# A fused attention and gating kernel on one core: a new order of its units, and a last output tile in two halves

## The chip, the core and the metric

The kernel runs on one core of a Trainium2 chip. A core has five engines that run side by side: TensorE (PE, matrix products, with PEld for the loading of its weights), VectorE (DVE), ScalarE (ACT), GpSimd (POOL) and SyncE (SP). Each takes its instructions in the order in which the program has them and waits at semaphores for the others. The metric is the device time of one execution in microseconds (us), lower is better: the median of three runs.

## The reference

Sinkhorn attention over blocks, and behind it a gated MLP whose gate mixes the tokens. There are 4 batches, 8 heads, 768 tokens in 8 blocks of 96, and a head size of 64; d_model is 512, d_ff 1024.

```python
P = sort_net                                   # (4, 8, 8, 8)
for _ in range(5):                             # Sinkhorn steps
    P = exp(P - max(P, -1)); P = P / sum(P, -1); P = P / sum(P, -2)
k_sorted = einsum('bhij,bhjcd->bhicd', P, k_blocks)     # the same for v
scores = q_blocks @ k_sorted.T / sqrt(64)      # inside each block of 96
attn = softmax(scores) @ v_sorted              # -> x, (4, 768, 512)

h = relu(x @ w_in); u, v = h[..., :512], h[..., 512:]
v_n = (v - mean(v)) / sqrt(var(v) + 1e-6)
v_s = einsum('ts,bsd->btd', w_spatial, v_n) + b_spatial
out = (u * v_s) @ w_out                        # (4, 768, 512) float32
```

## The kernel before

The whole kernel is one program of units, small functions that each issue one piece of work: for most of them the matmuls into one or two PSUM banks and the copy that empties them. A string, `ORDER`, lists the units with their arguments, and `run` calls them one by one. The schedule is manual: each engine gets its instructions in the order of the string, and only semaphores hold it up. So the string sets, for every engine, what stands behind what.

The arguments of a unit are, in this order, the PSUM bank (0 to 3 stand for the bank pairs 0-1, 2-3, 4-5 and 6-7; 10 to 17 stand for the single banks 0 to 7), for units with a choice the engine that copies (A is ACT, D is DVE, P is POOL), and then the batch, the head pair and so on. The units that matter here:

- `DM:bank:n:w` issues n matmuls of w columns on a zero tile, whose results nobody reads. They stand at the start, where PE has nothing else to do.
- `SK:n` is one Sinkhorn step (ACT's exponential, then DVE); the last one also turns P into `p_t`. `MC` makes `spread` on ACT, `MA` and `MB` make the mask on DVE. `PR` multiplies `spread` and `p_t` into PSUM; `P0` (batch 0, DVE) and `PD` (the others, POOL) multiply that by the mask into `pd`, a matrix per head that mixes the blocks.
- `L:q`, `L:k`, `L:v`, `L:wv` and so on load inputs, on POOL's queue, in order. `LH` and `QC` bring half of q of batch 0 over ACT's queue.
- `KT`, `VT` mix k and v with `pd` and turn them; `QT`, `QQ` turn q; `VB` turns the mixed v of batch 0 back into `vb`. For later batches `VM` mixes v into `vm`, and `VC` moves it into `vb` by small DMAs.
- `SC` makes scores and their exponential (ACT), `AT` the weighted sum of v and its division by the row sums (DVE, lines 505 and 506). `XT` turns the result for the MLP, on PE; `XD` does that by a DMA.
- `VP`, `UP` are the two halves of `x @ w_in`, with a ReLU; `ST`, `LN`, `LA` normalise v (DVE, ACT, DVE). `WT`, `WW` turn w_spatial (one or two chunks). `SP` mixes the tokens, DVE adds the bias into `z`, `GT` multiplies by u. `OP`, `OE`, `OS` make, copy and store an output tile.
- `CK` and `CF` check that no Sinkhorn sum left the range in which the quick form holds, and `LF` loads that flag on every engine. After `IF` stands the rest of the quick path; the other branch computes everything in a general form and is not run here.
- In the last batch `SH`, `GH` do `SP`, `GT` in narrower pieces, and `OH:bank:b:n:c0:c1`, `OI`, `OJ` make, copy and store the columns c0 to c1 of one output tile of 128 tokens. `OJ` ends in S or A for SP's or ACT's DMA queue.

The front of the program, up to the first `VP`, handles the Sinkhorn steps and the attention of batch 0; from there on, units of neighbouring batches are interleaved, so that matmuls of the MLP of one batch stand between the attention units of the next.

## Time and profile before

| | |
|---|---|
| three runs | 153.0, 153.16, 153.27 us; median 153.16 |
| the profiled execution | 154.13 us, of which 152.3 us from the first to the last instruction (the span) |
| PE busy | 143.7 us (94% of the span) |
| DVE, ACT, POOL busy | 114.7 (75%), 85.0 (56%), 42.3 us (28%) |
| chain that ended last | PE 83%, DVE 10%, DMA 2% |
| HBM traffic | 24.78 MB read, 6.29 MB written |

Rows of the timeline have the start in us, the duration in us, the engine, the line of the kernel, the operation, what it writes and from what, the shapes, the count, and in brackets how long the engine was idle before it and what ended that. Rows of the chain have start, duration and what ran. Rows of the waits have who waited for whom, the total in us, how many times, and the longest. Rows of the groups have a count, then busy us and the mean ns of one, then the idle time before them.

### The profile page before, as it was taken

The page shows a single profiled execution, that of the slowest core. Times are in us where ns is not written, and L with a number is a line of the kernel's source. Part 1 is how long each engine was busy: PE and PEld are TensorE (multiplying, and loading weights), DVE is VectorE, ACT ScalarE, POOL GpSimd, SP SyncE. Part 2 cuts the span into 40 slices and gives each one's busy share as a digit, 9 for nine tenths or more (in the row PEclk, how much of TensorE's full clock was granted, in tenths as well). Part 3 has the DMA queues.
Part 4 walks back from the last instruction along what each step waited for, and adds up shares of the span by engine and source line. Part 5 has one row for each costly group of instructions (what it writes and reads, how often), then busy time and mean ns, then how long its engine had stood idle before and what let it go on. Part 6 is the DMA issues. An engine that isn't in the chain of part 4 may idle for free.

```text
span 152.3 us, 4112 instructions
## 1 busy us (share of the span) xinstructions
PE 143.7 (94%) x1687; PEld 95.9 (63%) x1687; DVE 114.7 (75%) x264; ACT 85.0 (56%) x122; POOL 42.3 (28%) x46
## 2 busy tenths in 40 slices
PE   6786999989999999999999999999999999999991
PEld 2175867764687565965786674657875546764760
DVE  1789889966978773969992785988936989886742
ACT  4274999875889806788879055776240141340040
POOL 7400997092000004625000039200000620003630
PEclk9999999999999999999999999999999999999999
DMA  3999999999999990799993989300075024019356
GB/s 102 255 204 204 185 190 205 208 214 237 240 257 205 204 185 8 118 127 197 202 163 75 230 218 285 69 0 4 0 223 126 0 108 167 0 50 403 115 189 229
DMA packets 30695, 24.38 MB, mean 160 GB/s; under 512 B 10384, under 2 KB 27792, under 8 KB 30672
## 3 DMA queue, kind: packets, MB, share of 16 engines
q0 software_dynamic: 14432, 12.19, 50.6%
q1 hardware_dynamic: 14864, 9.92, 24.5%
q10 hardware_dynamic: 1376, 1.97, 3.8%
q8 instruction: 14, 0.23, 0.6%
q14 instruction: 9, 0.07, 0.2%
HBM read 24.78 MB, written 6.29 MB: 204 GB/s over the span
## 4 chain that ended last, share of the span: by engine, by line
PE 83%; DVE 10%; DMA 2%; issue 1%; ACT 1%; DVEq 0%
PE ps L619 15%; PE ps L564 14%; PE ps L607 14%; PE ps L645 10%; PE ps L675 5%; PE ps L498 5%; PE ps L452 4%; PE ps L393 4%; PE ps L695 3%; PE ps L420 3%; PE ps L528 2%; PE ps L324 2%; DVE x_sb L506 2%; DMA p_all<-in_sort_net_dram 2%; PE ps L411 1%
## 5 line engine op out<-in xcount | busy, mean ns | idle before, releaser
L636 POOL TENSOR_TENSOR gt<-z,u_sb 128x768 bf16<-128x768 f32 x9 | 14.6, 1637 | 70.1 <-DVE z L625 27.9
L457 ACT ACTIVATE ex_all<-ps 96x768 bf16<-96x768 f32 x32 | 23.9, 805 | 5.0 <-PE ps L452 4.6
L619 PE MATMUL ps<-wspT,v_sb 128*128 128x384 bf16 x144 | 24.9, 326 | 0.0
L564 PE MATMUL ps<-w_in_sb,xT 128*128 128x512 bf16 x96 | 23.4, 380 | 0.0
L607 PE MATMUL ps<-xT,w_in_sb 128*128 128x384 bf16 x128 | 23.1, 326 | 0.0
L506 DVE TENSOR_TENSOR x_sb<-ps,rec_all 96x512 bf16<-96x512 f32 x32 | 22.0, 686 | 1.1
L625 DVE TENSOR_TENSOR z<-ps,b_bc 128x768 f32<-128x768 f32 x12 | 11.4, 953 | 13.1 <-PE ps L619 13.1
L619 PEld LDWEIGHTS <-v_sb 128*128 128x128 bf16 x144 | 13.7, 98 | 8.7
L127 ACT ACTIVATE v_sb<-ps 128x512 bf16<-128x512 f32 (+1 forms) x15 | 9.9, 657 | 15.9 <-DVE bad L722 8.7
L581 DVE BATCH_NORM_STATS2 stats<-v_sb 128x6 f32<-128x512 bf16 x24 | 16.2, 674 | 1.7 <-ACT v_sb L127 1.5
L607 PEld LDWEIGHTS <-w_in_sb 128*128 128x128 bf16 x128 | 12.1, 98 | 7.9
L645 PE MATMUL ps<-w_out_sb,gt 128*128 128x256 bf16 x144 | 16.9, 273 | 0.0
L121 ACT COPY o_sb<-ps 128x1024 f32<-128x1024 f32 (+1 forms) x10 | 8.8, 882 | 12.9 <-DVE z L681 9.0
L127 ACT ACTIVATE u_sb<-ps 128x768 bf16<-128x768 f32 x12 | 9.7, 809 | 10.3 <-PE ps L607 10.3
L645 PEld LDWEIGHTS <-gt 128*128 128x128 bf16 x144 | 13.9, 98 | 2.1
L564 PEld LDWEIGHTS <-xT 128*128 128x128 bf16 x96 | 8.4, 98 | 8.5
L498 PEld LDWEIGHTS <-ex_all 96*128 96x128 bf16 x256 | 10.7, 97 | 3.6 <-issue 0.6
L498 PE MATMUL ps<-vb,ex_all 96*128 96x65 bf16 x256 | 11.8, 193 | 0.2 <-DVE x_sb L506 0.2
L291 POOL TENSOR_TENSOR pd<-mask,prep_sb 128x512 bf16<-128x512 bf16 x6 | 6.6, 1103 | 14.4 <-ACT prep_sb L121 9.6
L688 POOL TENSOR_TENSOR gt<-z,u_sb 128x512 bf16<-128x512 f32 (+1 forms) x5 | 5.2, 1046 | 18.4 <-DVE z L681 18.4
L121 ACT CAST vm<-ps 128x768 bf16<-128x768 f32 x9 | 7.1, 807 | 4.8 <-PE ps L420 4.7
L235 PE MATMUL ps<-warm 128*128 128x256 bf16 (+1 forms) x34 | 8.1, 400 | 1.3 <-DVE warm L209 1.3
(100 smaller groups left out, 208.6 us busy)
## 6 DMA issues: line engine op xcount, KB each, us to landing
out_dram<-o_sb SPq DMA_DIRECT2D x8, 512.0 KB, 3.4
v_in<-in_v_dram POOLq DMA_DIRECT2D x4, 768.0 KB, 13.3
k_in<-in_k_dram POOLq DMA_DIRECT2D x4, 768.0 KB, 11.1
vb<-vm SPq DMA_DIRECT2D x24, 99.0 KB, 4.4
q_in<-in_q_dram POOLq DMA_DIRECT2D x3, 768.0 KB, 25.3
ws_in<-in_moe_w_spatial_dram POOLq DMA_DIRECT2D x2, 576.0 KB, 17.8
w_in_sb<-in_moe_w_in_dram POOLq DMA_DIRECT2D x2, 512.0 KB, 12.4
q<-in_q_dram ACTq DMA_DIRECT2D x1, 768.0 KB, 4.6
```

Of the source, the lines that this page charges most:

```text
L121: nc.scalar.copy(out=out, in_=in_)
L127: nc.scalar.activation(out=out, in_=in_, func=AF.Relu)
L457: nc.scalar.activation(out=e_tile(b, hp, ih).rearrange("p h (x g) -> p h x g", g=G), in_=t[0:BLK, :, 0:HW].rearrange("p h (g x) -> p h x g ...
L498: nc.tensor.matmul(t[:, hh, ii * VW:ii * VW + D + 1], lhsT=e[:, c:c + 128], rhs=vb[b % 2][:, ih * NI + ii, 2 * hp + hh, 0:D + 1], start=Tr ...
L506: nc.vector.tensor_mul(out=x_sb[:, hp].rearrange("p i (h d) -> p h i d", h=2), in0=tv[:, :, :, 0:D], in1=_raw_ap(rec, 0, [rec.ap[0], [NI, ...
L564: nc.tensor.matmul(t[:, x, :], lhsT=st["xT", b][:, n // 3, kc, (n % 3) * 128:(n % 3 + 1) * 128], rhs=w_in_sb[:, kc, DH:DFF], start=(kc == ...
L581: nc.vector.bn_stats(out=stats, in_=st["v_sb", b, n])
L607: nc.tensor.matmul(t[:, x, 0:HW], lhsT=w_in_sb[:, kc, mc * 128:(mc + 1) * 128], rhs=st["xT", b][:, ih, kc, :], start=(kc == 0), stop=(kc = ...
L619: nc.tensor.matmul(t[:, x, 0:HW], lhsT=st["v_sb", b, n][:, mc * 128:(mc + 1) * 128], rhs=wspT[:, 3 * x:3 * x + 3, n, :], start=(n == 0), s ...
L625: nc.vector.tensor_add(out=z.rearrange("p (x c) -> p x c", x=2), in0=t[:, :, 0:HW], in1=b_bc.rearrange("p (x c) -> p x c", x=2),)
L636: eng.tensor_mul(out=gt, in0=st["z", b, mc], in1=u)
L645: nc.tensor.matmul(t[:, x, c:c + w], lhsT=st["gt", b, mc][:, (n0 + x) * 128:(n0 + x + 1) * 128], rhs=w_out_sb[:, mc, c:c + w], start=(mc = ...
```

## The change

All units stand in a new order, with other PSUM banks and, for many, another engine for the copy. Counted over the string: 16 of 16 `UP` are copied by ACT (12 before), 10 of 22 `VP` units by DVE (7 before), 5 of 6 `WT` by DVE, where before there were two `WT` and two `WW`, all on ACT; one `KT` and one `VM` go from DVE to ACT, one `VB` from ACT to DVE (all four are there now). The first `DM` units have 13 matmuls of 256 columns and 4 of 512, in place of 12 of 512; those between q's turning and `PR` have 8 of 512 and 9 of 256, in place of 18 of 256 (and 4 behind `PR`, now none). On POOL's queue k of batch 1 is loaded ahead of v of batch 1, and both, with q of batch 1, ahead of the first two `PD`. Four of the `VC` DMAs of the last batch and two more output stores go over ACT's queue.

The last output tile's columns 0 to 256 are made, copied and stored as 0 to 128 and 128 to 256, the first copied by ACT and stored over ACT's queue, the second by DVE and SP. The function for `VP` gets an argument `parts`, and a unit `VH` that uses it is added, but no unit of the order calls it.

The new string, cut to its front and its end, and the rest of the diff:

```diff
-S0 CO DM:10:5:512 IV:0 LH:A:0 TB SK:0 DM:10:3:512 L:q:0:4:8 BH ID SK:1 SK:2 IV:2 QC:A:0 DM:10:4:512 QC:A:1 SK:3 MA
-L:v:0:0:8 MC SK:4 QQ:0:A:0:0 DM:12:10:256 DM:12:8:256 L:k:0:0:8 QT:12:D:0:3 PR:13 L:v:1:0:8 MB DM:10:4:256 P0:0:2
...
-OJ:3:5:256:512:S OJ:3:4:0:256:A
+S0 CO DM:10:6:256 L:q:0:4:8 L:v:0:0:8 LH:A:0 TB SK:0 BH ID SK:1 SK:2 DM:10:7:256 DM:10:2:512 QC:A:0 QC:A:1 SK:3
+DM:10:2:512 SK:4 QQ:0:A:0:0 MC IV:0 MA QT:12:A:0:3 DM:13:8:512 MB DM:13:9:256 PR:10 P0:0:2 P0:2:4 P0:4:6 P0:6:8
...
+OH:10:3:4:128:256:0:4 OI:D:3:4:128:256 OJ:3:5:256:512:S OJ:3:4:0:128:A OJ:3:4:128:256:S
...
-    def u_VP(ps, eng, b, *tiles):
+    def u_VP(ps, eng, b, *tiles, parts=1):
...
-            for kc in range(KC):
-                nc.tensor.matmul(
-                    t[:, x, :],
...
+            for c in range(0, DH, DH // parts):
+                for kc in range(KC):
+                    nc.tensor.matmul(
+                        t[:, x, c:c + DH // parts],
...
+    def u_VH(ps, eng, b, *tiles):
+        u_VP(ps, eng, b, *tiles, parts=2)
```

## The prediction

> **What bounds the kernel now.** I read the windows view first, cut where the work changes character, then the waits of VectorE (DVE) in the first cut, then the timeline and the chain at the places that the new order touches.

> The windows view, with busy us and (in brackets) instructions of each engine, then clock, DMA share and GB/s:

> ```profile
> core 0: us, PE busy (x) PEld busy (x) DVE busy (x) ACT busy (x) POOL busy (x), PEclk, DMA share, GB/s
> 12.98:33.11 20.13, 18.39 (x431) 14.91 (x430) 18.24 (x35) 17.04 (x24) 13.21 (x15) 1.00 1.27 199
> 33.11:148.94 115.83, 115.81 (x1185) 75.96 (x1181) 88.11 (x189) 62.09 (x89) 24.50 (x20) 1.00 0.69 149
> 148.94:152.25 3.31, 0.00 (x0) 0.00 (x0) 0.43 (x2) 0.00 (x0) 0.00 (x0) 1.00 0.59 212
> ```

> The kernel has three parts. From 33.11 to 148.94 us TensorE (PE) is busy 115.81 of 115.83 us: no order of the same matmuls can shorten that stretch, and a bad one can only open holes. Before it lies a front of 33.11 us, in which PE is held up by others; behind it 3.31 us in which the last copies and stores land. A gain must come from the front or the end.

> In the front the Sinkhorn steps run first, to 12.4; they are the same in both kernels. In the cut behind them three columns lie close together: of 20.13 us DVE is busy 18.24, ScalarE (ACT) 17.04, PE 18.39. A busy PE there holds many short matmuls that overlap, so I take DVE, which cannot overlap much, as the engine that paces it. Its last copies before the steady stretch are at the very end of the cut:

> ```profile
> 32.23 0.33 PE L528 MATMUL ps<-ident,x_sb 96*128 96x96 bf16 x4 [0.45 <-issue]
> 32.60 0.56 DVE L123 COPY xT<-ps 128x768 bf16<-128x768 bf16 x1 [0.43 <-PE ps L528]
> 33.11 3.19 PE L564 MATMUL ps<-w_in_sb,xT 128*128 128x512 bf16 x14
> ```

> So DVE ends the front at 33.16, PE begins its long run at 33.11, and DVE was idle 20.13 - 18.24 = 1.89 us on the way. The waits of DVE in this cut, and the instructions that stood behind them:

> ```profile
> DVE vb L123 <- PE ps L411: 0.5, 2, 0.3
> DVE xT L123 <- PE ps L528: 0.4, 1, 0.4
> DVE rec_all L505 <- PE ps L452: 0.4, 1, 0.4
> DVE vt_all L123 <- PE ps L393: 0.3, 1, 0.3
> 15.60 0.69 DVE L123 COPY vb<-ps 96x1024 bf16<-96x1024 bf16 x1 [0.29 <-PE ps L411]
> 17.43 1.81 DVE L123 CAST kt_all<-ps 128x768 bf16<-128x768 f32 x2
> 19.43 1.28 DVE L123 COPY vb<-ps 96x1024 bf16<-96x1024 bf16 x2 [0.19 <-PE ps L411]
> 21.66 0.35 PE L452 MATMUL ps<-qT,kt_all 64*128 64x96 bf16 x8 [0.21 <-DVE x_sb L506]
> 22.01 0.20 DVE L505 RECIPROCAL rec_all<-ps 96x8 f32<-96x8 f32 x1 [0.40 <-PE ps L452]
> 46.95 1.02 DVE L123 COPY xT<-ps 128x768 bf16<-128x768 bf16 x2
> ```

> **Term 1, the front.** First what the order shows on DVE in the first half of the front, before (pd is the block-diagonal mix matrix, vt_all and kt_all the mixed v and k, vb the turned v, rec_all and x_sb the normalised output of one attention unit AT):

> ```order
> L279 TENSOR_TENSOR pd<-mask_89,ps 128x256 x4
> L123 CAST vt_all<-ps 128x768
> L123 COPY vb_97<-ps 96x8x2x64
> L123 CAST vt_all<-ps 128x768
> L123 CAST kt_all<-ps 128x768 x2
> L123 COPY vb_97<-ps 96x8x2x64 x2
> L505 RECIPROCAL rec_all<-ps 96x8
> ```

> Before, one vb copy stands between the vt_all casts and two behind the kt_all casts. The same place on DVE after:

> ```order
> L280 TENSOR_TENSOR pd<-mask_89,ps 128x256 x4
> L124 CAST vt_all<-ps 128x768
> L124 COPY vb_97<-ps 96x8x2x64 x2
> L124 CAST vt_all<-ps 128x768
> L124 CAST kt_all<-ps 128x768 x2
> L124 COPY vb_97<-ps 96x8x2x64
> L506 RECIPROCAL rec_all<-ps 96x8
> ```

> Now two stand between the vt_all casts, and one is left before the first AT; the fourth vb copy (ACT did it) comes later on DVE. In the second half DVE loses one kt_all cast to ACT and gains one xT copy. Its work changes by -1.81/2 + 1.28/2 + 1.02/2 = -0.91 + 0.64 + 0.51 = +0.2 us. The mask's reduction and cast, and the q copy that leaves DVE, lie ahead of 12.98.

> Then the idle time. Only 0.40 + 0.27 (the vt_all row, 0.3) + 0.19 + 0.43 + 0.29 of it has a named cause. The 0.40 was a ring: the scores' matmuls at 21.66 waited for banks that the AT before held, and the next AT stood behind them in PE's queue. In the new order the first three ATs go to banks 6-7, 4-5 and 0-1, and two of them wait in PSUM while DVE works on the first: I strike 0.40. The vt_all wait is covered by the second vb copy: 0.27 off. The vb wait of 0.19 goes too, for its matmuls no longer come right behind two casts with nothing between. The 0.29 stays, since the first vb still hangs on ACT's cast of the first vt. The 0.43 comes from a hole of 0.45 us in PE's own stream ("issue") that no unit explains; I strike half, 0.2. Left are 1.89 - 0.40 - 0.27 - 0.19 - 0.2 = 0.83 us, and DVE would end the front at 12.98 + 18.24 + 0.2 + 0.83 = 32.25 in place of 33.16: 0.9 earlier. Ends of the range: nothing gained (the waits come back elsewhere and the 0.2 is added: +0.2), or no idle time at all: 31.4, 1.7 earlier.

> One thing cuts this short. The heads' v of the second batch goes through vm and eight small DMAs into vb, and the first AT of that batch needs four of them (the second row is the fourth DMA alone, issued at 31.75):

> ```profile
> 29.52 5.41 SPq L433 DMA_DIRECT2D vb<-vm  x8
> vb<-vm SPq DMA_DIRECT2D x1, 99.0 KB, 7.9
> 42.29 0.48 PE ps L498 x16
> 97.08 0.86 PE ps L564 x4
> 97.95 1.30 PE ps L607 x8
> ```

> The fourth landed at 31.75 + 7.9 = 39.65, and the AT ran at 42.3, so nobody waited. In the new order that AT stands behind six VP tiles (0.86 each), two SC and one UP (1.30), some 7.0 us after the run starts: at 32.25 + 7.0 = 39.3. The last vm copy also comes some tenths earlier, with the front. I let this eat 0.3: the front is worth **-0.6 us**.

> **Term 2, the steady stretch.** Counted by unit from the two orders, the matmuls are the same in number and shape, but for the last tile. There 4 of 256 columns become 8 of 128. A row for 128-column matmuls with their own 128-column weights each (the transposes of the spatial weights) gives their pace, 0.67/12 = 0.056, so 0.45 in place of 4 x 0.109 (16 of 256 columns in 1.75): +0.01.

> ```profile
> 41.62 0.67 PE ps L541 x12
> 74.23 1.75 PE ps L645 x16
> ```

> Everything else here is hidden while PE has its next operands. More copies go to ACT (all 16 of u; busy 62.09 of 115.83) and to DVE (88.11): both have room. Four vb DMAs of the last batch are now issued by ACT (about 0.68 each, 5.41/8), at a place where ACT has only casts behind them; three output stores join them. The front's loads keep their bytes. The order of POOL's queue shows v0 ahead of k0 in both kernels; what changes is k1 ahead of v1, and that k1, v1 and q1 are no longer queued behind the two pd products that wait for ACT. The transfers run at 199 GB/s through the front, so the stream of loads has no gap to close and I cost that at nothing; cover gone, it would be a few tenths at the first use of v1. Sum of term 2: **0**, to +1 where a margin fails (rivals).

> **Term 3, the end.** The chain's last pieces, the stores' issues and their landing, and the copies' sizes:

> ```profile
> 149.01 0.42 DVE o_sb L123
> 148.16 1.65 ACTq L707 DMA_DIRECT2D out_dram<-o_sb  x3
> DMA to landing us min/median/max: 1.8/2.2/2.7
> L123 DVE COPY o_sb<-ps x5: 424/425/693, 146.4 to 149.0; 128x256 f32<-128x256 f32 x4, 128x512 f32<-128x512 f32 x1
> ```

> Now: the copy of 256 columns ends at 149.43, ACT issues its store at 149.47 (the third of the row, 0.34 long), it lands 1.8 later. The order of ACT's last rows before:

> ```order
> L121 COPY o_sb<-ps 128x512 x2
> L707 DMA out_dram<-o_sb 128x512
> L121 COPY o_sb<-ps 128x512
> L707 DMA out_dram<-o_sb 128x256 x3
> L803 UNCONDITIONAL_BRANCH
> ```

> The last three stores stood together, with no copy between them. After, the same rows of ACT from the third copy on:

> ```order
> L122 COPY o_sb<-ps 128x512
> L712 DMA out_dram<-o_sb 128x256 x2
> L122 COPY o_sb<-ps 128x128
> L712 DMA out_dram<-o_sb 128x128
> L808 UNCONDITIONAL_BRANCH
> ```

> ACT now copies the first half itself behind its second store; DVE copies the other half, and SP stores it. DVE's 693 for 512 and 425 for 256 columns put 128 at about 0.29 (an estimate on their line): 149.01 + 0.29 = 149.30, SP's issue at 149.34 in place of 149.47. ACT's half comes out at the same moment. **-0.1 us**, from -0.2 to +0.4 (landing in 2.2, the median, with five stores in flight, not 1.8).

> **The sum.** -0.6 + 0 - 0.1 = -0.7. The profiled execution took 154.13 with a span of 152.3; it would be 153.4, span 151.6. It lies 0.97 above the median of the three runs (153.16); against that the forecast is **152.5 us**. About 0.2% (0.3 us) is what a measurement of this kernel can tell from no change.

> **Rivals.** *A, slower: the warm-up matmuls come too late or too few.* The rows:

> ```profile
> PEclk9999999999999999999999999999999999999999
> 1.28 5.30 PE L235 MATMUL ps<-warm 128*128 128x512 bf16 x12 [1.28 <-DVE warm L209]
> 7.85 0.53 PE L324 MATMUL ps<-ident,q_in 128*64 128x128 bf16 x12 [1.27 <-ACT q_in L121]
> 9.04 2.14 PE L235 MATMUL ps<-warm 128*128 128x256 bf16 x18
> 12.40 0.35 PE L265 MATMUL ps<-p_t,spread 32*128 32x32 bf16 x8 [0.76 <-DVE p_t L260]
> ```

> The first twelve took 5.30/12 = 0.44 per 512 columns, the later ones 2 x 2.14/18 = 0.24: PE's pace doubled between 6.6 and 9.0, though the granted clock (first row, by slices of 3.8 us) reads full from the start. The new order has 5376 columns ahead of q's transposes, not 6144, so they end at 1.28 + 5.30 x 0.875 = 5.9, and PE then idles 1.9 us to 7.85, not 1.27. Behind the transposes it puts 6400 columns ahead of the matmuls (L265) that P waits for, not 4608: at the fast pace 2.97 us, ending near 12.4, just when p_t is ready; at the slow pace 5.52 us and slower transposes, ending near 16. If PE is still slow then, the whole front moves by up to 3.5 us, and by about 1.2 if the pace doubles halfway; I take +1.7 on the forecast, 154.2. It decides as soon as the dummies end after 12.5. For it: the margin is nil. Against: 4.6 us of work is still a long stretch. [...] Chance **0.14**.

> What spread, the other operand of these matmuls, waits for, and the first product behind them:

> ```profile
> 8.75 0.60 ACT L226 COPY spread<-ident 32x512 bf16<-32x512 bf16 x1
> 10.51 1.41 ACT L121 COPY qT<-ps 128x1536 bf16<-128x1536 bf16 x1
> 12.98 1.41 DVE L279 TENSOR_TENSOR pd<-mask,ps 128x256 bf16<-128x256 bf16 x4
> ```

> A smaller delay of the same matmuls is sure: ACT now makes spread (L226, 0.60) behind the copy of qT (1.41), not ahead of the last exponential; 10.51 + 1.41 + 0.60 = 12.5, against the 12.40 at which p_t released PE. P's first product (L279) started at 12.98 before, behind the mask's cast, so at most 0.1 of it shows.

> *B, no change: the front's gain is handed back.* DVE keeps its 1.89 us of idle time in other places, or the first AT of the second batch waits for vb until 39.65 and longer: 153.1. [...] Chance **0.20**.

> The rows for rival C, z's sums, the first and the last of the check's instructions, and its matmul:

> ```profile
> L625 DVE TENSOR_TENSOR z<-ps,b_bc 128x768 f32<-128x768 f32 x12 | 11.4, 953 | 13.1 <-PE ps L619 13.1
> 119.17 0.41 DVE L721 TENSOR_REDUCE ends<-rec_all 96x1 f32<-96x256 f32 x1
> 120.85 0.14 DVE L722 TENSOR_SCALAR bad<-ends 32x1 bf16<-32x1 f32 x1
> 124.85 0.10 PE ps L735
> ```

> *C, slower by holes in the steady stretch.* The check of the sums (CK, short DVE instructions from 119.17 to 120.99) and its matmul (CF) stood 3.8 us apart. Now DVE adds z of the last SP (0.96), runs CK (1.8), and PE passes OP (1.75) and UP (1.30) meanwhile: 3.05 against some 3.0 with the latency. DVE behind by half a us there stops PE for as long, as would the six normalising products ahead of the next-to-last batch's SP, where I count 0.3 of room. Two such holes of 0.5 and a front that gains nothing: 154.1, and slower by any sum over 1.0. Chance **0.12**.

> **How the numbers follow.** The forecast, 152.5, has 0.54; its own range is 151.9 (the front at 1.2) to 153.0. Low end of all: 151.9; the high end takes in rivals C and the middle of A: 154.2. Faster: 0.54 x 0.95 + 0.20 x 0.25 = 0.56. Slower: A 0.14, most of C 0.11, a quarter of B 0.05 = 0.30. The same: 0.14.

> **What would show it.** Right: PE's long run (first L569) begins near 32.4, DVE's idle time from the first pd product to there is near 0.9, PE has no hole behind it, and the last store is issued 0.1 earlier after the last matmul. Wrong: dummies that take 0.44 per 512 columns behind the transposes (A); a wait of PE on vb, or a start at 33 (B); waits of PE on DVE near CF or before an SP (C).

## The result, and the profile after

The first comparison gave the changed kernel 154.72 us (median of four runs, 154.44 to 155.07) against 153.13 for the kernel before: 1.0105 times as long, with a 95% interval of 1.0082 to 1.0128. The forecast was 152.5, the upper end of its range 154.2. More executions on another chip, below, put the change nearer to nothing (1.0029, 0.9996 to 1.0062). Why the two differ is half of the story: with the new order, PE has half clock for 3.4 us at the head of some executions (3 of 4 in the first comparison, 4 of 11 in the second) and not of the others. Two executions far above the rest (156.0 us of the changed kernel, 156.3 us of the one without a branch) are left out of all counts and medians here and below.

The profiled execution of before was late at its head: its first exponential, which waits for the Sinkhorn input, began 0.72 us later than in another execution (at 3.31, not 2.59), and all behind it followed. So that other one (same kernel, span 151.2) is compared here.

**The head.** The timeline of the changed kernel, warm-up, q's transposes, warm-up, and the spread matmuls on which P hangs:

```profile
1.28 4.41 PE L236 MATMUL ps<-warm 128*128 128x256 bf16 x17 [1.28 <-DVE warm L210]
7.17 0.53 PE L325 MATMUL ps<-ident,q_in 128*64 128x128 bf16 x12 [1.48 <-ACT q_in L122]
9.09 4.16 PE L236 MATMUL ps<-warm 128*128 128x512 bf16 x16 [0.33 <-issue]
13.18 0.36 PE L266 MATMUL ps<-p_t,spread 32*128 32x32 bf16 x8
```

The same places of the kernel before:

```profile
1.28 4.51 PE L235 MATMUL ps<-warm 128*128 128x512 bf16 x12 [1.28 <-DVE warm L209]
7.14 0.53 PE L324 MATMUL ps<-ident,q_in 128*64 128x128 bf16 x12 [1.35 <-ACT q_in L121]
8.33 2.14 PE L235 MATMUL ps<-warm 128*128 128x256 bf16 x18
11.68 0.35 PE L265 MATMUL ps<-p_t,spread 32*128 32x32 bf16 x8 [0.76 <-DVE p_t L260]
```

The spread matmuls come at 13.18, not 11.68, and nothing but the warm-up ahead of them on PE holds them up (p_t was ready at 11.66, spread at 11.76). By windows (PE busy first; the granted clock is the third figure from the end), the changed kernel:

```profile
8.00:10.00 2.00, 1.67 (x27) 1.07 (x29) 1.31 (x7) 0.50 (x3) 0.00 (x0) 0.68 1.31 204
10.00:12.00 2.00, 2.00 (x6) 0.68 (x5) 1.76 (x9) 2.00 (x3) 0.00 (x0) 0.50 1.31 203
12.00:14.00 2.00, 1.54 (x18) 1.17 (x17) 0.49 (x3) 0.45 (x1) 0.00 (x0) 0.97 1.31 204
```

A mean of 0.68, 0.50 and 0.97 is half clock for 1.28 + 2.00 + 0.12 = 3.4 us, from 8.7 to 12.1. The 16 warm-up matmuls took 4.16 us; in a kernel below, at full clock, the same 16 take 2.66.

**The rest, by parts.** From the spread matmuls to the long run of matmuls (first VP), to the first OH, to the end of the last matmul, to the end; the changed kernel, then the kernel before:

```profile
13.18:33.11 19.93, 18.43 (x437) 15.24 (x436) 18.18 (x36) 15.98 (x23) 11.35 (x13) 1.00 1.28 206
33.11:143.24 110.13, 109.71 (x1146) 72.83 (x1150) 82.91 (x183) 60.24 (x86) 25.03 (x19) 1.00 0.73 147
143.24:148.97 5.73, 5.53 (x38) 3.17 (x35) 3.11 (x8) 1.76 (x3) 1.41 (x2) 1.00 0.30 112
148.97:153.27 4.30, 0.01 (x1) 0.00 (x0) 0.31 (x2) 0.27 (x1) 0.00 (x0) 0.86 0.64 226
```

```profile
11.68:32.03 20.35, 18.96 (x441) 15.44 (x440) 18.73 (x37) 17.04 (x24) 12.85 (x15) 1.00 1.28 201
32.03:142.49 110.46, 109.93 (x1146) 72.94 (x1151) 84.90 (x182) 60.34 (x86) 23.44 (x18) 1.00 0.72 149
142.49:147.85 5.36, 5.36 (x34) 3.03 (x31) 3.22 (x8) 1.75 (x3) 1.40 (x2) 1.00 0.45 170
147.85:151.17 3.32, 0.00 (x0) 0.00 (x0) 0.45 (x2) 0.00 (x0) 0.00 (x0) 1.00 0.60 213
```

Head +1.50, front -0.42, steady stretch -0.33, last tiles +0.37, end +0.98: +2.1 us. The front did become shorter, and the head and the end took 2.85 us for the 0.75 that it and the steady stretch gave.

**The end.** The chain of waits of the changed kernel at that place:

```profile
144.36 0.09 DVE gt L693
144.46 2.56 issue
...
147.19 0.70 DVE o_sb L124
147.89 0.04 issue
147.93 0.61 PE ps L700 x4
```

"issue" is DVE with nothing to execute, and it comes right behind its branch (`IF`): its next instruction follows the branch by 2.64 us, before by 1.84. So DVE copies the third output tile at 147.19, 3.95 us after the first OH; before it was 2.84 after, and PE ended the wait:

```profile
145.33 0.69 DVE L123 COPY o_sb<-ps 128x512 f32<-128x512 f32 x1 [1.42 <-PE ps L695]
```

PE needs that bank again: from one matmul's start to the next 0.48 us pass there in place of 0.11, a hole of 0.37 us (the windows view has 0.20 idle, since the ends of matmuls are modelled). And the stores come late and all at once. The DMA engines (last figure GB/s) are idle, then full to the end:

```profile
147.50:148.00 0.50, 0.30 (x4) 0.12 (x2) 0.50 (x2) 0.00 (x0) 0.00 (x0) 1.00 0.06 16
148.00:148.50 0.50, 0.50 (x7) 0.45 (x7) 0.50 (x2) 0.00 (x0) 0.00 (x0) 1.00 0.00 0
150.50:151.00 0.50, 0.00 (x0) 0.00 (x0) 0.00 (x0) 0.00 (x0) 0.00 (x0) 1.00 1.11 387
```

Last, the program's final waits on SP (start of the first and of the last), changed kernel, then before:

```profile
L837 SPq EVENT_SEMAPHORE  x8: 27/28/28, 151.9 to 152.3; - x8
```

```profile
L832 SPq EVENT_SEMAPHORE  x5: 28/28/28, 149.3 to 150.2; - x5
```

In the semaphore records there is one wait for each of the eight semaphores that the stores share, always in the same order, 0.06 us apart. Eight stores leave the last one at the end of that order. The ninth takes the first place: when it lands at 151.87, seven waits still follow, to 152.31. The last of all landings, the eighth store's, is at 152.05, so 0.24 us are lost to the order. Before, the last wait came 0.02 behind the last landing.

### The profile page after: what moved, and what is told of

It is laid out like the page before. It is cut to its first block, busy times and chain, and to the rows that moved or that the text cites. A ratio compares the mean times of both kernels' runs of the same rounds, so it can differ in the third digit from the quotient of the medians.

```text
span 153.3 us, 4096 instructions
## 1 busy us (share of the span) xinstructions
PE 143.5 (94%) x1682; PEld 96.6 (63%) x1691; DVE 112.0 (73%) x265; ACT 84.8 (55%) x123; POOL 44.2 (29%) x47
## 4 chain that ended last, share of the span: by engine, by line
PE 80%; DVE 8%; issue 4%; ACT 3%; POOL 2%; ACTq 0%; DVEq 0%
PE ps L624 15%; PE ps L566 14%; PE ps L612 14%; PE ps L650 10%; PE ps L499 5%; PE ps L453 4%; PE ps L394 3%; PE ps L236 3%; PE ps L421 3%; PE ps L680 3%; PE ps L325 2%; PE ps L529 2%; POOL gt L693 2%; PE ps L535 1%; PE ps L412 1%
## 5 line engine op out<-in xcount | busy, mean ns | idle before, releaser
L641 POOL TENSOR_TENSOR gt<-z,u_sb 128x768 bf16<-128x768 f32 x10 | 16.4, 1644 | 69.7 <-DVE z L630 64.8
L566 PE MATMUL ps<-w_in_sb,xT 128*128 128x512 bf16 x88 | 22.7, 380 | 0.4
L128 ACT ACTIVATE u_sb<-ps 128x768 bf16<-128x768 f32 x16 | 12.8, 809 | 12.2 <-PE ps L740 8.7
L122 ACT COPY o_sb<-ps 128x1024 f32<-128x1024 f32 (+2 forms) x12 | 10.0, 842 | 12.3 <-PE ps L700 9.3
L650 PEld LDWEIGHTS <-gt 128*128 128x128 bf16 x144 | 13.9, 98 | 2.4
L122 ACT CAST vm<-ps 128x768 bf16<-128x768 f32 x10 | 7.7, 806 | 10.0 <-PE ps L421 10.0
L122 ACT CAST kt_all<-ps 128x768 bf16<-128x768 f32 x11 | 8.4, 801 | 4.9 <-PE ps L394 4.9
L128 ACT ACTIVATE v_sb<-ps 128x512 bf16<-128x512 f32 (+1 forms) x12 | 7.9, 670 | 5.3 <-PE ps L566 5.1
L292 POOL TENSOR_TENSOR pd<-mask,prep_sb 128x512 bf16<-128x512 bf16 x6 | 6.5, 1096 | 13.2 <-ACT prep_sb L122 9.1
L236 PE MATMUL ps<-warm 128*128 128x256 bf16 (+1 forms) x33 | 8.6, 440 | 1.6 <-DVE warm L210 1.3
## 6 DMA issues: line engine op xcount, KB each, us to landing
k_in<-in_k_dram POOLq DMA_DIRECT2D x4, 768.0 KB, 13.1
w_in_sb<-in_moe_w_in_dram POOLq DMA_DIRECT2D x2, 512.0 KB, 12.4
```

The costliest lines, as they stand in the source:

```text
L122: nc.scalar.copy(out=out, in_=in_)
L128: nc.scalar.activation(out=out, in_=in_, func=AF.Relu)
L236: nc.tensor.matmul(t[:, 0, 0:int(w)], lhsT=warm[:, 0:128], rhs=warm[:, 0:int(w)], start=True, stop=True)
L566: nc.tensor.matmul(t[:, x, c:c + DH // parts], lhsT=st["xT", b][:, n // 3, kc, (n % 3) * 128:(n % 3 + 1) * 128], rhs=w_in_sb[:, kc, DH + c ...
L641: eng.tensor_mul(out=gt, in0=st["z", b, mc], in1=u)
L650: nc.tensor.matmul(t[:, x, c:c + w], lhsT=st["gt", b, mc][:, (n0 + x) * 128:(n0 + x + 1) * 128], rhs=w_out_sb[:, mc, c:c + w], start=(mc = ...
```

## The experiments

Theory: three separate causes, half-clock windows (head), a late copy behind DVE's branch (end), a ninth store (end). The rival to each stands in the expectations. Diffs are against the changed kernel, except where said.

### How much of it is chance: both kernels again

> The kernel before, unchanged, run again for its profile, the spans of several executions and their granted clock. Its timed runs lie at 153.0 to 153.27 us, but its profiled execution took 154.13 (span 152.3). Theory 1: that one execution was a slow one by about 1 us at its start or its end; other executions should show spans near 151.3 and the same steady stretch, and the microsecond should be found in the head (the long run of matmuls starting before 33.1) or behind the last matmul (under 3.31 us). Rival: the profiled execution is like the others and a profiled run costs 1 us by itself; then every span of it is near 152.3.

Measured: spans of 151.2 to 151.7 in twelve executions; the profiled one was the fastest. The first theory holds: the missing 1.08 us lie ahead of the long run (from 32.03, not 33.11), 0.72 of them in the head (spread matmuls at 11.68, not 12.40).

> The changed kernel, unchanged, in more executions. Theory of the clock: the windows in which the clock is granted begin at a point of their own in every execution; where a window of 3.41 us covers the idle time of PE between 5.7 and 7.2 us, the next one is granted half, the granted clock of the run is 0.982 to 0.987 and its time is 1.1 to 1.3 us longer. So the times fall into two groups about 1.2 us apart, by the granted clock, and the better group lies near 154.0 to 154.4 (0.8 to 1.1 us above the kernel before, all of it at the end). Rival: the granted clock and the time have nothing to do with each other, and the times form one group around 154.7.

Measured: 1.0029 (0.9996 to 1.0062). By granted clock the executions split as said, but the better group lies lower than expected, at 153.59 and not at 154.0 to 154.4, and one of it (154.45) stands between the groups. Here and below, "half" counts those with a granted clock of 0.989 or less:

| kernel | executions | half | median half | median others |
|---|---|---|---|---|
| before (five chips, 129 in all; medians of the chip of the next row) | 129 | 11 | 154.61 | 153.32 |
| changed, again | 11 | 4 | 154.90 | 153.59 |
| changed, first comparison | 4 | 3 | 154.79 | 154.44 |
| before, 1.5 fewer warm-up matmuls | 12 | 6 | 154.13 | 153.37 |
| all kernels here with the changed kernel's own warm-up | 80 | 38 | | |
| all kernels here with four more warm-up matmuls | 30 | 0 | | |

So the first comparison met three half executions in four, and an execution of that kind costs some 1.3 us more. The others of the second are only about 0.3 us above the kernel before; the single other one of the first, 154.44, is not explained.

### The warm-up

```diff
-DM:10:2:512 SK:4 QQ:0:A:0:0 MC
+DM:10:6:512 SK:4 QQ:0:A:0:0 MC
```

> The changed kernel with four more warm-up matmuls of 512 columns ahead of q's transposes (the last group is 6 instead of 2). Theory (rival A of the prediction): after the change PE idles from 5.7 to 7.2 us, the clock is granted at half from 8.7 to 12.1 us, the warm-up behind the transposes therefore ends at 13.18 instead of under 12.4, and the spread matmuls start 0.78 us late. With PE busy to about 6.7 the clock should stay full: granted clock of the run near 1.0, spread matmuls at 12.4 to 12.5, the long run of matmuls from 32.4 instead of 33.1, time 0.6 to 0.8 us under the changed kernel. Rival: the half clock comes from something else than the idle time, and it stays; then the time is the same or up to 0.2 us longer.

Measured: 1.0068 (1.0055 to 1.0080), no half execution in six, spread matmuls at 11.81 and the long run from 31.69, earlier than expected (12.4 was where P was ready in the late execution of before):

```profile
8.92 2.66 PE L236 MATMUL ps<-warm 128*128 128x512 bf16 x16 [0.16 <-issue]
11.81 0.36 PE L266 MATMUL ps<-p_t,spread 32*128 32x32 bf16 x8 [0.23 <-ACT spread L227]
```

The same 16 matmuls take 2.66 instead of 4.16. The half window is gone, as expected. The time, 154.24, fell by 0.5 against the first comparison, but it is 0.65 above the others of the second (on another chip): these six runs show no gain over an execution that has no half window anyway, and why they are slower than those is open.

The other way round, in the kernel before:

```diff
-QC:A:0 DM:10:4:512 QC:A:1
+QC:A:0 DM:10:2:512 DM:10:1:256 QC:A:1
```

> The kernel before with 1.5 fewer warm-up matmuls of 512 columns ahead of q's transposes, so with the 5376 columns of the changed kernel instead of 6144, all else as before. Theory: PE's idle time ahead of the transposes grows from 1.35 to about 1.7 us, so more executions have a half-clock window behind the transposes: about 4 of 10 instead of 7 of 62, each 0.8 to 1.3 us longer at a granted clock of 0.982 to 0.989; the others are as before. Rival: it is the new order (four heads' transposes ahead, the warm-up behind them longer) and not the columns ahead that makes the half windows; then they stay at about 1 in 10.

Measured: 1.0034 (1.0014 to 1.0054), 6 of 12 half, where the kernel before on the same chip had 0 of 21. So fewer columns ahead of the transposes are enough to bring the half windows; it does not take the new order.

### The late copy

```diff
-OH:17:3:0:0:512:0:4 OI:D:3:0:0:512 OI:A:3:3:0:512 ... OJ:3:3:0:512:A OI:A:3:1:0:512
+OH:17:3:0:0:512:0:4 OI:A:3:3:0:512 ... OJ:3:3:0:512:A OI:A:3:0:0:512 OI:A:3:1:0:512
```

> The changed kernel with the copy of the third output tile (row block 0, 512 columns) on ACT instead of DVE. Theory: at the end of the changed kernel DVE has nothing to execute for 2.56 us behind its branch (144.46 to 147.03), so this tile is copied at 147.19 instead of 146.40 as before; its store and the next one go out 0.8 us later, all stores then queue on the DMA engines, and the end comes 0.75 us later. On ACT the copy should start near 146.15, the store at 146.75, PE's hole of 0.37 us ahead of the last tile but three is gone, and the time falls by 0.8 to 1.0 us. Rival: the late end comes from the split of the last tile (a ninth store, rows of 512 bytes); then the time changes by less than 0.2 us.

Measured: 1.0032 (1.0011 to 1.0053), 4 of 12 half, the others at 153.32. In its profile (no half window; it is the changed kernel up to its end):

```profile
31.79:141.96 110.17, 109.75 (x1145) 72.89 (x1150) 82.91 (x183) 60.22 (x86) 24.95 (x19) 1.00 0.74 149
141.96:147.34 5.38, 5.38 (x38) 3.16 (x35) 2.47 (x7) 2.34 (x4) 1.41 (x2) 1.00 0.44 168
147.34:151.32 3.98, 0.00 (x0) 0.00 (x0) 0.32 (x2) 0.27 (x1) 0.00 (x0) 0.78 0.52 178
```

The hole is gone (5.38), and the end is 0.32 shorter: 0.67 of the 0.8 to 1.0 expected. Without a half window the changed kernel would thus end at 141.96 + 5.73 + 4.30 = 151.99, against a median span of 151.5 for the kernel before. The times of this run, on another chip than the changed kernel's, show less: 153.32 against 153.59 without a half window, 154.44 against 154.90 with one.

The next kernel has no branch at all (the general path is left out):

```diff
-        with tc.If(st["beyond"] < 1, preferred_fallthrough_block=False, label="usual") as usual:
-            run(tail)
-        with usual.Else():
-            general_path()
+        run(tail)
```

> The changed kernel without the branch ahead of its last part (the general path for inputs out of bounds is left out, and its hint; the inputs here do not take it). Theory of the late copy: without the branch DVE has its next instruction at once; it copies the third output tile as soon as PE has made it, at about 146.1 instead of 147.2, the hole of PE of 0.2 to 0.4 us goes, and the last store lands under 2.8 us behind the last matmul instead of 3.08; time 0.7 to 1.0 us less than the changed kernel. Rival: DVE is held by something else (the stores, a semaphore), and the 2.4 us of idle time ahead of that copy stay; time the same within 0.2.

Measured: 1.0061 (1.0030 to 1.0092), 154.15 without half windows: no gain, so its expected time failed. The profiled execution (156.3 us) has full clock only from 13.9 us, so only its end is read:

```profile
147.58 0.69 DVE L124 COPY o_sb<-ps 128x512 f32<-128x512 f32 x1 [1.34 <-PE ps L700]
150.16:154.51 4.35, 0.00 (x1) 0.00 (x0) 0.31 (x2) 0.27 (x1) 0.00 (x0) 0.93 0.48 163
```

The copy waits for PE and for nothing else (2.79 behind the first OH), the hole is gone, and the last landing is 2.43 behind the last matmul instead of 3.08. But between the last of SP's final waits and the end of the span lie 1.48 us, not 0.96; most of the difference is POOL's first step of the ending, 0.44 us there and 0.09 in the changed kernel. Why is not settled.

What makes DVE go on so late? Tiny fills at its start change nothing but the place of all that follows in its program:

```diff
         nc.vector.memset(vt_all[:, :, S:], 0.0)
+        for _ in range(12):
+            nc.vector.memset(eps_tile, 1e-6)
```

> The changed kernel with 12 more tiny fills of a constant on DVE at the very start, where DVE is idle from 1.5 to 2.6 us. They cost no time themselves; they put all that follows 12 instructions further in DVE's program. Theory: DVE's late copy at the end is a matter of where its branch lies against the blocks of 8 KB in which its instructions are fetched (with 322 recorded instructions ahead of the branch, before, the fetch of what follows the branch comes at the branch itself and DVE goes on after 1.8 us; with 319, after the change, it comes 0.7 us later and DVE goes on after 2.6 us). Then 12 more move the fetch ahead of the branch again: the third output tile is copied when PE has made it, near 146.1 on the clock of the changed kernel's trace or 1.1 us behind the first copy's end on DVE's wait for PE, the hole of PE goes, and the time falls by 0.5 to 0.8 us. Rival: the place in the program does not matter, the branch takes 2.5 us as before and the time stays within 0.2 us.

> The changed kernel with 3 tiny fills on DVE at the start instead of 12, which brings the recorded instructions ahead of DVE's branch from 319 to 322, the number of the kernel before. If the place of the branch in DVE's program is what counts, and its position before was just far enough, DVE goes on some 1.7 us behind the branch, as before, in time for the third output tile (its copy waits for PE, no hole of PE), and the end is that of the kernel with 12 fills: 3.8 to 3.9 us behind the last matmul instead of 4.3. If 3 are too few, the copy stays 0.8 us late. Time against the changed kernel: 0.5 less in the first case, the same in the second.

Measured, 12 fills: 1.0064 (1.0050 to 1.0077), but five of six executions were half; those at 154.25, against 154.90 for the changed kernel's on another chip. 3 fills: 1.0017 (0.9983 to 1.0051), 7 of 12 half, at 154.45 (the changed kernel's two on that chip took 154.98 and 155.27); the others at 153.05, where the kernel before has 153.35. The copies, 12 fills and then 3:

```profile
146.11 0.69 DVE L124 COPY o_sb<-ps 128x512 f32<-128x512 f32 x1 [1.39 <-PE ps L702]
148.64:152.47 3.83, 0.00 (x0) 0.00 (x0) 0.30 (x2) 0.27 (x1) 0.00 (x0) 0.85 0.53 181
```

```profile
146.08 0.69 DVE L124 COPY o_sb<-ps 128x512 f32<-128x512 f32 x1 [1.39 <-PE ps L702]
148.61:152.53 3.92, 0.00 (x1) 0.00 (x0) 0.31 (x2) 0.27 (x1) 0.00 (x0) 0.93 0.52 179
```

DVE goes on 0.60 us behind the branch with 12 fills, 1.79 with 3 (before: 1.77 to 1.84 in four traces), and 2.50 to 2.64 with none (nine traces). So the place in the program decides, and three instructions make 0.7 us or more of difference. The DMA records show a packet of 8 KB of instructions that starts 0.67 to 0.71 us behind the branch where there are no fills, within 0.04 us of it with 3 fills and in the kernel before, and 2.0 us ahead of it with 12. In the changed kernel's trace it is the one packet of the DMA view between 144.9 and 145.2 us, behind the branch at 144.37:

```profile
DMA packets 1, 0.01 MB, mean 27 GB/s; under 512 B 0, under 2 KB 0, under 8 KB 0
q14 instruction: 1, 0.01, 11.4%
```

In the first two cases, fourteen traces, DVE goes on 1.8 to 2.0 us behind that packet's start. Whose instructions a packet holds, no record says: that DVE waits for this packet is an estimate from these times, and no run isolates it.

### The last tile

```diff
-OH:13:3:4:0:128:0:4 OI:A:3:4:0:128
-OH:10:3:4:128:256:0:4 OI:D:3:4:128:256 OJ:3:5:256:512:S OJ:3:4:0:128:A OJ:3:4:128:256:S
+OH:13:3:4:0:256:0:4 OI:D:3:4:0:256
+OJ:3:5:256:512:S OJ:3:4:0:256:A
```

> The changed kernel with the last output tile made, copied (DVE) and stored (ACT's queue) in one again, all else as changed. Theory of the late copy: the DMA engines still have the same bytes to store from 148.7 us on, so only the ninth store's own cost goes: the final waits on the store semaphores stand in a fixed order, and with nine stores the last but one is waited for first and seven waits of 0.06 us follow; time 0.2 to 0.4 us less. Rival (the split is what costs): 1.0 us less, last landing back at about 2.3 us behind the last matmul.

Measured: 1.0043 (1.0017 to 1.0068), 5 of 12 half, the others at 153.51. Its end is 3.96 us, 0.34 shorter, and the last wait follows the last landing at once. That is inside the expected 0.2 to 0.4. The half execution's span (152.8) is 0.46 under the changed kernel's. By times, on another chip, the half executions gain 0.3 (154.60 against 154.90) and the others hardly anything (153.51 against 153.59).

And the split alone, in the kernel before (the diff the other way, with before's bank 14):

> The kernel before with only the last output tile of 256 columns made, copied (ACT and DVE) and stored (ACT's and SP's queue) as two of 128. The prediction gave this -0.1 us (-0.2 to +0.4). Theory from the traces: the last matmul ends where it did, the copies end 0.1 us earlier, but the ninth store takes the first place in the order of the final waits, so that seven waits of 0.06 us follow its landing, and two stores at once land 2.1 to 2.5 us behind their issue instead of 1.8: 0.3 to 0.6 us slower. Rival: the prediction's, -0.2 to +0.1.

Measured: 1.0034 (1.0023 to 1.0046), no half executions. The end is 0.65 longer than the 3.32 before, and the eight waits are there:

```profile
147.85:151.82 3.97, 0.00 (x0) 0.00 (x0) 0.31 (x2) 0.27 (x1) 0.00 (x0) 0.77 0.52 178
L833 SPq EVENT_SEMAPHORE  x8: 28/28/28, 150.4 to 150.9; - x8
```

Of the 0.65, 0.42 are the order of the waits, and 0.23 the last landing, 2.57 behind the last matmul instead of 2.34. The last store did leave earlier, by 0.06 (at 148.34, with the last matmul at the same 147.85). It bought nothing.

### Both ends, and all together

> The changed kernel with both edits of its end: the third output tile copied by ACT, and the last tile made, copied and stored in one. If the end is made longer by the late copy (0.6 us alone) and by the ninth store (0.4 alone, by its landing and by the order of the final waits), and by nothing else, the last landing comes back to 2.36 us behind the last matmul and the end of the span to 3.3 to 3.4 us behind it, as in the kernel before; time 1.2 to 1.4 us under the changed kernel, still in two groups by the granted clock. Rival: something else of the end is left, and the span ends over 3.6 us behind the last matmul.

Measured: 0.9972 (0.9947 to 0.9998), 3 of 12 half at 153.97, the others at 152.92. That is 0.9 and 0.7 under the changed kernel's two groups on the same chip, not the 1.2 to 1.4 expected. No hole; the end is 3.81 us, so the rival holds: 0.5 is left. Its stores land 2.3 to 2.7 us after their issue, where the kernel before has 1.8 to 2.2:

```profile
DMA to landing us min/median/max: 2.3/2.5/2.7
```

In the landing records, 15 of the 16 parts of each store arrive as before, and one arrives 0.5 to 0.6 later, in all six last stores. DVE is still late behind its branch here, and a packet of 8 KB of instructions lies in that stretch, at 147.53. The two other kernels in which ACT copies the third tile show such a laggard too, 0.4 to 0.5 us (that copy alone) and 0.6 to 1.0 (the next kernel). In the kernel before and with 3 fills, where the packet comes earlier, it is a part of a single store, by 0.5 to 0.7 us, and the stores behind it lag by 0.3 at most. In the changed kernel, whose last stores are issued only behind the packet, none lags. With 12 fills there is no packet there and no laggard.

> The changed kernel with the new order kept, both edits of its end, four more warm-up matmuls of 512 columns ahead of q's transposes, and ACT's copy of spread ahead of the last exponential again. If the half clock and the end are all that made the change slower, and the new order of the front is worth 0.3 to 0.5 us as the traces have it, this is faster than the kernel before: 152.6 to 152.9 us, granted clock 0.99 or more in all runs, spread matmuls at 11.7, the long run of matmuls from 31.6. Rival: the gain of the front is handed back in the steady stretch or by the stores; then it equals the kernel before within 0.2 us.

Measured: 0.9963 (0.9935 to 0.9990), median 153.08 of twelve, none half. Faster than before (153.53 on that chip, 153.32 without its half executions), by less than expected: its end is 3.87.

> The changed kernel's order with what the runs found wrong put right: four more warm-up matmuls of 512 columns ahead of q's transposes and ACT's copy of spread ahead of the last exponential, the last tile made, copied and stored in one, and 12 tiny fills at DVE's start, so that the fetch behind its branch comes early and DVE copies the third output tile itself. Theory: no half-clock window, spread matmuls at 11.7, the long run of matmuls from 31.6, the span ending 3.3 us behind the last matmul: span 150.6 to 150.9, time 152.3 to 152.6, 0.6 to 0.9 us under the kernel before. Rival: the earlier end of the front is handed back in the steady stretch (0.25 us of it was, in the two kernels with more warm-up); if all of it is, the time is that of the kernel before less 0.3 us at most.

Measured: 0.9975 (0.9960 to 0.9991), median 153.00 of twelve (152.27 to 153.22) against 153.33; none half. By parts:

```profile
11.95:31.97 20.02, 18.23 (x437) 15.23 (x437) 18.61 (x38) 16.20 (x24) 11.14 (x13) 1.00 1.29 205
31.97:142.31 110.34, 109.86 (x1146) 72.88 (x1150) 82.89 (x183) 60.23 (x86) 25.22 (x19) 1.00 0.73 149
147.67:150.95 3.28, 0.00 (x1) 0.00 (x0) 0.45 (x2) 0.00 (x0) 0.00 (x0) 0.96 0.60 215
```

The end is back at 3.28. The front is 0.33 shorter than before and the steady stretch 0.12, but the head is 0.27 later (0.17 of that in the Sinkhorn steps, where the first loses 0.14), so the span gains 0.2 and the median 0.33: half of what was expected. The kernel before is beaten, narrowly.

### The changed kernel twice more

> The changed kernel once more, for the profile of an execution without a half-clock window (eleven executions split 4 to 7). From the traces so far such an execution should show the spread matmuls at 11.8, the long run of matmuls from 31.7, a hole of 0.2 to 0.4 us at the end, and 4.3 us behind the last matmul: span 151.8 to 152.0. Their times (median 153.59) say 151.8. If the span is below 151.7, part of what the traces count as lost at the end is not lost in those executions.

> The same kernel again, with the same expectation: spread matmuls at 11.8 and a span of 151.8 to 152.0 without a half-clock window, 13.2 and 153.2 with one.

Both were half executions (spread matmuls at 13.26 and 13.28, spans 153.4 and 153.2; time 155.27 and 154.98), as the expectation has them, but no execution of the changed kernel without a half window was profiled. For it the pieces sum to a span of 151.99 (above), 0.5 over before's median; the executions show 0.3. Those 0.2 us stay open.

## Why the prediction was wrong, point by point

Two steps failed. The warm-up was taken to be long enough (rival A at 0.14): in 38 of 80 executions with this warm-up it was not; the granted clock went back to half (for 3.4 us in the profile), which made them some 1.3 us longer. And term 3, put at -0.1, measured +0.98 with a hole of 0.37 ahead of it. Together they outweigh the front's gain.

- **Term 1, the front (-0.6): near in size, not in its terms.** From the spread matmuls on, the front is 0.42 shorter (0.51 in the profile without a half window), and the steady stretch gives 0.04 to 0.33 on top. But DVE's idle time from the first pd product to the long run was to fall by 1.06 us and its work to grow by 0.2; by the same cut the idle time fell by 0.22 (1.51 to 1.29), the work by 0.08, and the first pd product came 0.12 sooner behind the spread matmuls. So the size is in part luck. The waits of DVE there, changed kernel and before:

```profile
DVE vb L124 <- PE ps L412: 0.7, 2, 0.5
DVE xT L124 <- PE ps L529: 0.3, 1, 0.3
```

```profile
DVE vb L123 <- PE ps L411: 0.5, 2, 0.3
DVE rec_all L505 <- ACT ex_all L457: 0.4, 1, 0.4
DVE vt_all L123 <- PE ps L393: 0.3, 1, 0.3
```

  The waits of rec_all and vt_all went (in this execution of before, ACT's exponential ended the first, not the matmuls of the ring). The vb wait did not go but grew by 0.2, and xT's, 0.4 in the late execution of before, is 0.3. The long run begins at 33.11 in the profile only because the head is late; without a half window it begins at 31.79.
- **Rival A (0.14): what happened, and priced too low in chance.** The dummies at half pace stood where it said, and 154.2 was a little under what such executions take (154.6 to 155.3). The failed step is the judgement that 4.6 us of work was "still a long stretch": no trace then showed how much work is enough. The kernel before itself had half windows in 11 of 129 executions, so 0.13 us more idle time ahead of the transposes was not a margin that one could take. With 38 of 80 executions hit, the chance should have been near a half.
- **Term 2 (0): right.** No wait at CK or CF shows, nor at vb's DMAs; rival C did not happen. If anything the stretch is shorter. (Two more output stores go over ACT's queue, not three; nothing hangs on that.)
- **Term 3 (-0.1, to +0.4): wrong, +0.98 and a hole of 0.37.** DVE's half of the copies ended when it said, ACT's 0.2 later, so that the last store left no earlier behind the last matmul than before. Three more things were missing: the ninth store's place in the final waits (0.42 with the split alone, 0.24 here), the longer landing, and the branch. The hole at `OI:D:3:0` needed DVE's idle time of 1.42 ahead of that copy to be read as what it was: cover of a branch that took 1.8 us, with PE ready only just after. That row was in the trace.
- **The baseline.** 154.13 against a median of 153.16 was taken as an offset. It was a late head in that one execution; the offset was right in size.
- **Spread made later on ACT (at most 0.1): right.** 0.10, where no half window hides it: with more warm-up, p_t is ready at 11.66 and spread at 11.76.

## What to carry to other kernels

Ask how busy PE is around each idle stretch of the head (here 1.72 us of 3.41 lost the full clock, and 1.86 kept it), and measure often enough to see two groups; four runs can fall on one side. Cutting the last tile finer did not pay here, since it added a store: count the stores against the semaphores that the ending waits for, and see whether the stores' transfers, not the copies, end last. A branch late in the program can have a price that moves with the number of instructions ahead of it (here 0.6 to 2.6 us), so leave the first work behind it to an engine with cover.

## What the runs showed of the hardware

- In the changed kernel's trace the clock record has full clock for 3.41 us from 5.29, then half clock for 3.41 us from 8.71 to 12.12. In the eight traces in which the clock fell back, the half window began at 7.97 to 8.71 us, at another time in each. PE was busy 1.72 us in the window ahead of the half one, half of it, and still lost the clock; in the kernel before, 1.86 us in the window from 4.85, by the trace's clock record, kept it. The changed kernel's row, then before's:

```profile
5.29:8.71 3.41, 1.72 (x38) 1.08 (x38) 2.43 (x13) 1.97 (x4) 2.19 (x3) 1.00 1.31 203
4.85:8.27 3.41, 1.86 (x29) 0.93 (x26) 2.43 (x12) 2.10 (x5) 0.67 (x1) 1.00 1.31 204
```
